# Attention times value by head: two banks of one double, one normalisation, and a new planned order

## The chip, the core and the metric

The kernel runs on one core of a Trainium2 chip. TensorE (PE) multiplies matrices into PSUM, VectorE (DVE) and ScalarE (ACT) work elementwise and can read PSUM, GpSimd (POOL) works on SBUF, and SyncE (SP) issues most DMAs. Each engine runs its own list of instructions in order and waits on semaphores for the others. The metric is the device time of one execution, in microseconds; the median of three runs of the kernel before is 265.42.

## The reference

Two layers, one behind the other. The first is attention with a block mask: 4 batches, 8 heads, 768 positions, head size 64. The mask keeps blocks of 32 x 32: neighbours, the first and last block row and column, and three drawn blocks for each block row. The second is x @ w_in, then h * sigmoid(beta * h), then @ w_out, on 3072 tokens.

```python
scores = scale * np.matmul(q, k.transpose(0, 1, 3, 2))
scores = np.where(mask, scores, -1000000000.0)
scores = scores - np.max(scores, axis=-1, keepdims=True)
attn = np.exp(scores)
attn = attn / (np.sum(attn, axis=-1, keepdims=True) + 1e-09)
out = np.matmul(attn, v)
...
h = x @ w_in
g = h * (1.0 / (1.0 + np.exp(-beta * h)))
return (g @ w_out).astype(np.float32)
```

## The kernel before

**Units.** Heads are taken in pairs, 16 pairs in all (x), four for each batch. The queries of a batch are cut into a tile of 256 and one of 512 (n), so there are 32 units of one pair and one tile. A unit has score steps ("sc", line 602): each fills one *double* of PSUM, a tile "sc" of two banks with 512 columns each, one bank for each head. Head 0 stands in rows 0 to 63 of kX and qX and head 1 in rows 64 to 127, so a score product uses 64 of PE's rows, and those of the two heads stand in the list one behind the other. ACT takes the exponential of a whole double into "et" ("ex", line 621), and DVE multiplies it by the mask ("mk", line 626). The first four units (N_PEMASK) have the mask added on PE instead, by products of shut_qk and onehot. There are four doubles, eight banks.

**Attention times value (add_tail, line 653).** For each 128 queries and each head, six products of 128 rows and 65 columns (64 of v and a column of twos that yields the sums) add up in one bank ("mm" is a single bank, half of a double). Two groups of 128 queries times two heads share a bank. So a unit of 256 queries has one such step "av" of 24 products, and one of 512 has two ("half"). DVE then takes the reciprocal of the four sums ("rc", line 679) and multiplies ("nm", line 682) into xst. From there xst is transposed into x, in the first eight units and the last pair by PE, otherwise by a transposing DMA of SP.

**The second layer (add_moe, line 741).** Groups of 256 or 512 tokens: "hp" is x @ w_in (four products of 512 or 256 columns), "th" a tanh on ACT, "gm" the gate on DVE. Five of the groups are done with fewer products through sums and differences of halves ("sg", "pr", add_mixed, line 824), the first one and the last differently sized.

**Loads.** k, q and v come by SP's DMAs into st, are cast to half precision by DVE or POOL (add_cast, line 523), and k and q are then transposed: by PE for the first four pairs, by a DMA of SP (line 544) for the other twelve.

**Order.** The order of all this is written out. STEPS (line 43) lists node numbers in the order of emission, each with its engine letter and the slots of the buffers that it takes. in_steps (line 163) reads it. A token such as 1x192V2 puts one zero matmul of 192 columns into bank 2; besides these, four stand in emit_first (line 390). A token such as 176P5:171 puts two steps together (in_halves, line 317): each is done as products of 64 rows, the first node with rows 0 to 63 and the second with rows 64 to 127 in turn; at the later token of the pair the row halves change over. Between the two an empty instruction of POOL is told to wait for the last product of each half, and the second run waits for it. Where a POOL cast is emitted, it is told to wait for the DVE instruction emitted last before it (line 1021).

**Banks.** Tile dependencies are kept for each double; class Banks (line 204) takes away those between different banks of a double.

Of the kernel before, what the change touches and what calls it, by code (L numbers as in the profile page):

```python
# [10 lines left out]
FP32 = mybir.dt.float32  # L11
# [12 lines left out]
class Node:  # L24


    def __init__(self, kind, eng, dur, lat, emit, deps=(), take=(), use=(), moved=0,
# [11 lines left out]
        self.first, self.mark = False, None  # L39
# [4 lines left out]
0D 1V2 1x192V2 1P4 30S3 34S5 16S6 12S1 13G0 17G4 38S 44S0 31D3 39G 32P7 35D5 1x192V2 36P0 24S 20S 48S6  # L44
3A 1x192V2 8P6 33D2 6P1 7D 25G 21G 1V2 18P3 14P7 15D0 37A 2A 9A 19A 2x192V6 89P2 90Ab 1x256V1 40P0
1x256V1 78P1 79A4 41D 1x256V1 91P3 93P0 4P4 22P2 26P3 94Ad 45G3 49G6 46P5 27D 5D 82P0 2V3
1x128V3 50P4 23A 92A5 80P1 58S3 54S7 28S5 72G 29G3 42S4 64S1 73G 74G 47D1 51D 83A7 81Aa 1x448V0
100P3 101A3 102P2 103A6 104P0 105A0 52S8 53G1 59D0 68S3 55D3 75G 76G 77G 56P3 57D3 60P2 61D 84P6
115P1 116A9 113P2 111P0 65D0 66P7 43D0 85D3 95P3 112A4 62S6 86D0 67D 87P2 88D2 191P0 194P3 114A7
192Ae 96De 97D0 188P2 69D5 106P3 70P0 71D 63G2 10P1 98P2 11D 99D 107D0 108D4 195A1 193D 196D  # L50
185P3 189A3 186A6 211P0 1V2 1x256V2 182P2 1x320V3 117P2 118D3 119D0 2V3 1x448V3 109P2 197P3
120P3 212Aa 214P0 183A4 208P2 190D 110D 121D 131P3 198A0 122P6 137P7 209Ac 217P2 187D 199D 184D
200P2 123A1 132A3 124D1 143P6 133D 210D 215A9 138A2 201D2 202D4 128P1 140P3 125P0 218A2 134P4
146P2 203P5 129A1 216D 139D 213D 130D 126A3 127D 144A4 145D 135A6 147A0 141A5 220P3 221A0 238G4
234G6 235S 223P0 136D 155P4 156A3 204D8 205D 142D 158P5 159A6 224A6 164P7 206P3 161P6 162A2 148D
219D 149P2 157D 160D 222D 150A3 245P0 246A5 152P4 167P5 168A1 165A0 153A4 225D 163D 226P6 251P0
252A8 207D2 151D 248P1 249Ae 169D 229P5 227Da 166D 228D1 285P3 154D 257P0 170P4 258A1 253D 230De
231D 247D 250D 176P5:171 288P1 260P0 259D 286A2 287D 365D 366D 361D 236D0 239S 242G5 171P 254P3
172P:177 289A4 279P1 261Ad 294P0 177P 178P:173 243S 237S0 271S2 255Ab 256D 291P3 295Ac 262D
282P0 173P 280A9 296D 290D 240D5 281D 241S 179P 292A0 293D 263P7 283A7 266P3 272G2 232P1 284D  # L60
297P2 300P0 180A0 174A1 233A 402P2 367D 264Da 362D 265D3 244G1 267Dh 268D 269P1 298D1 299D0
301Dc 302D 405P3 270D 303P0 304D 403Aa 363D 364D 404D 411P1 408P2 406A6 274S4 277S6 305S5 273S3
308S8 311S7 275D4 276S 427S2 313P1 409A7 410D 412A8 413D 314A3 315D1 306G3 322P6 319P7 323A0
324D 407D 278G3 312G2 309G0 428G4 417P2 414P1 418A9 415Ae 416D 320A5 321D 331P0 316P1 317A3
332A1 318D 333D 328P4 329A0 330D 334P5 335A4 336D 325P3 326A2 435P3 436A0 438P0 337P2 340P4 419D
420P5 439Ab 444P3 441P0 338A6 327D 369D0 437D 341A3 346P3 339D 421D8 349P2 422D0 352P5 445Ac
442A2 447P0 450P3 342D 343P4 350A6 446D 347A2 443D 351D 423P2 348D 440D 355P3 448A4 449D 424Dd
425D 451A3 452D 353A3 354D 430S4 433S0 307S2 310S 181S 175S 466P3 460P0 358P2 344A4 434G0 431G3
345D 453P5 456P4 356A1 461Ad 463P0 357D 359A5 454Dh 360D 475P1 467Aa 469P3 457D3 455D1 464A3
375P5 472P0 376P 470A8 476A9 429S1 432S 485P3 491P1 372D 373D 468D 462D 458D 471D 378P4 379P  # L70
473A1 488P0 492Ac 497P1 486Ab 465D 474D 477D 481P7 478P6 489A7 494P0 498A6 500P1 495Ad 501A9
368D 377D0 380D 482D1 370D 487D 386P 597P0 598Ae 387P:383 479D2 480D3 493D 483D 499D 496D 502D
591P3 594P1 383P 604P0 617S1 620S6 426S1 459S 592A2 595Aa 607P3 608A8 605A0 384P 385A 618D1 490D
506P3 503P2 625P3 621D5 371D 623S4 638S5 388A1 626A9 610P0 611Ad 641S0 639G2 374D 504D9 505D1
389P 390P 628P3 629A3 507Dg 508D 631P1 632A5 652P0 653A1 381D 382D 593D 392P 393P 596D 599D 627D
612D 600P6 646P0 644S7 619S0 659S3 484S 642G0 394D 633D 601D7 602D4 606D 647Aa 509S 513P74:510
649P1 650A4 510P 511A4 622S 667P0 662S1 665S2 680S5 640S2 683S6 686S8 668A2 670P1 516P6 609D
660D6 391D 395P 671A6 630D 648D 669D 517A3 663G4 512D0 518D 528P0 522P1 525P2 519P3 529A1 530D
514A5 515D 643S 523A6 524D 526A1 520A0 672D 527D 673P3 688P0 674Ae 396P 531P4 397A 689Ab 661S3
664S 398S 681G1 682S1 521D 634P3 635D5 654D 636D1 532A3 690D 533D 691P3 694P0 692Ac 695A5 613P2  # L80
614Db 684D0 651D 615D2 675D 537P3 538A3 701P3 704P2 702A8 645G1 703D 705A7 534P1 549P0 550A4
543P6 546P5 540P7 539D 535A6 552P2 706D 624G3 666G2 551D 544A5 547A2 541A3 553A1 536D 545D 555P3
542D 685S 603S0 616S 399S 401S 714P3 707P0 548D 655P4 556A5 708Ad 676P5 715A1 720P0 696D 554D
557D 717P1 677Dc 558D0 561D 678D2 564P6 565P 656Db 657D4 808P2 718A6 811P1 721A3 814P0 567P7
809A2 693D 697P5 568P 812A0 815Aa 566A0 817P1 687D0 560D 563D 562D 698De 699D0 823P2 820P0 818A9
559D 709D 572P 569D 710P3 575P 824A5 821Ac 833P0 858S4 861S6 658S 679S 722D 716D 711Dc 712D3
836P2 839P1 834Ad 576P 719D 571D 723P1 573P 810D 400S 577D1 724Dc 864S8 637S 725D1 840A7 837Ae
845P2 848P0 849A1 842P1 570D 581P 582P 574D 578P 846A3 579P 866P2 713S 891S5 813D 825D 841D 822D
892D2 869P0 843A4 872P1 867Ab 847D 583D 726S 700S 730P7 727P5 873A8 733P3 819D 816D 844D 826P2
829P4 731A1 728A5 870A6 580D 584P 850D 874D 729D1 894S0 895G5 859G0 732D 734A3 585P 827D7 828D3  # L90
735D 830Df 831D 860S2 838D 835D 586D 590S 589S 878P0 875P1 739P4 736P7 879A5 881P0 876Aa 880D
877D 862G3 863S 897S4 899P1 924S6 587S 927S7 893S3 588S 740A2 745P6 737A6 882A9 741D 748P4 746A4
900A0 749A3 751P0 752A1 738D 851P1 747D 871D 905P3 760P32:742 906Ac 750D 852Dc 902P2 742P 911P3
903A2 753D 883D 853D2 761A2 743A4 908P2 854P1 909A4 762D 868D 855D5 744D 856D 907D 910D 772P0
773A0 912Ad 766P3 763P5 757P2 764A1 769P6 754P7 865G3 913D 928G4 925G3 765D 914P2 774D 1013P0
832S1 857S 896S 926S0 930S1 929S 1038S2 767A3 768D 758A4 759D 884P3 887P2 770A6 755A5 915A7
1014A1 1028P2 1029Aa 771D 756D 1019P3 885D6 886D0 1016P0 781P3 904D 888Db 889D 784P2 1020Ab
1022P3 1017A5 785P:782 1025P2 1058P0 782P 1023A9 1026A6 1049P3 775D0 901D 778D 1015D 780D 916D
917P4 920P5 783A0 776D 1027D 779D 789P 786D 918D0 919D2 921D4 922D 1050Ae 1059A4 1021D 1030D
1060D 1051D 1046P3 1047A3 792P:790 1052P2 1053Ac 890S 1041S6 1071P0 1061P3 790P 1055P2 793P  # L100
1062A2 777D 1018D 1044S8 923S 932P7 947P6 1072A0 1056A7 1074P0 962P4 933A1 948A2 1075Ad 788D
1024D 1042D2 934D0 1057D 1073D 1048D 1034P7 1031P1 938P5 963A4 949D 950P6 944P0 1032D9 931G0
794D1 1033D2 964D 935P4 787D 798P 799P 953P1 951A5 952D 939A0 940D 1054D 1035D3 936A2 945A5 937D
1036D 946D 1076D 791A 800D 804S 959P4 941P6 954A6 1039G4 1045G1 898D2 955D 1040S1 1043S 805S
956P2 795P 960A4 961D 942A1 957A6 1083P2 943D 1077P3 1080P0 796P 1084Aa 1078A6 958D 971P4 968P2
1081Ab 969A0 1063D 980D0 970D 1082D 797D 977P1 974P6 1064P5 972A1 965P2 801P 975A0 976D 978A5
# [40 lines left out]
HOP = 60.0  # L147
# [911 lines left out]
```

## Time and profile before

| | |
|---|---|
| runs, us | 265.65, 265.42, 264.58 (median 265.42) |
| profiled execution, span | 265.9 us |
| ACT, exponentials | 144, 139.7 us busy |
| DVE, masks | 132, 83.0 us busy |
| PE, x @ w_in of 512 columns | 304 of 128 rows, 70.4 us busy |
| PE, attention times value | 1152, 42.6 us busy |
| DMA, mean | 138 GB/s |

How to read the rows: a group's row has the engine, the operation, what it writes and reads, the shapes, the count, busy time and the mean length of one in ns, and after the bar the idle time of the engine before them with what ended it. For PE the shape begins with rows * columns of the array that are used. A row of the timeline has its start and its length in us; consecutive equal instructions are merged. Matmuls overlap, so the length of one (269 ns, say) is longer than the distance from one to the next. PEld is the loading of weights. A row of the table by stretch has the stretch, its length, the busy time of PE, PEld, DVE, ACT and POOL, the granted clock, the DMA share and GB/s. In the chain, "PE sc L198" is PE's matmuls (line 198 is a recording helper), and the number behind the start is how long the chain ran there.

### The profile page before, as it was taken

To read this page: it belongs to the slowest core of one execution; us is meant where nothing else is said; L and a number is where in the kernel's file an instruction comes from. 1 tells how busy PE (TensorE), PEld (TensorE's weight loads), DVE (VectorE), ACT (ScalarE), POOL (GpSimd) and SP (SyncE) were. 2 spreads that over 40 slices of the span, in tenths; PEclk is the share of its full clock that TensorE was granted. 3 is DMA by queue.
4 is the path that set the end of the run, shared out by engine and by line. 5 is a ranking of instruction groups with operands and counts; after the bars stand their busy time and mean duration, and the time that the engine had idled before them with its cause. 6 is when DMAs were issued, how large, how long until landed. Compare 5 with 4: busy or idle time off the path is not lost.

```text
span 265.9 us, 7061 instructions
## 1 busy us (share of the span) xinstructions
PE 257.2 (97%) x2899; PEld 168.6 (63%) x2899; DVE 227.7 (86%) x477; ACT 211.2 (79%) x284; POOL 35.6 (13%) x56
## 2 busy tenths in 40 slices
PE   8999999999998999799999999999999999999995
PEld 3575674644455875546776446766567886568884
DVE  4277999999998899599999889999879789778872
ACT  5699999889997989798976999994868876674331
POOL 4482000116020111140002103001200000000000
PEclk9999999999999999999999999999999999999999
DMA  6899994699739579625441597910504103110042
GB/s 186 285 248 232 200 215 161 138 284 258 150 59 271 138 182 271 158 67 184 127 99 55 138 257 179 237 25 0 129 11 121 22 2 120 31 42 0 5 156 79
DMA packets 50131, 36.70 MB, mean 138 GB/s; under 512 B 29732, under 2 KB 46644, under 8 KB 50100
## 3 DMA queue, kind: packets, MB, share of 16 engines
q1 hardware_dynamic: 46368, 32.06, 46.2%
q0 software_dynamic: 3664, 4.19, 9.3%
q8 instruction: 22, 0.36, 0.6%
q14 instruction: 9, 0.07, 0.1%
q10 hardware_dynamic: 68, 0.01, 0.0%
HBM read 27.27 MB, written 6.29 MB: 126 GB/s over the span
## 4 chain that ended last, share of the span: by engine, by line
PE 72%; DVE 9%; DMA 6%; ACT 5%; issue 4%; SPq 1%; POOL 1%; DVEq 0%; ACTq 0%; POOLq 0%
PE sc L198 72%; DMA qX<-s 4%; DVE et L198 4%; ACT et L198 3%; DMA st<-in_v_dram 2%; ACT t_sb L198 1%; DVE w_mix L198 1%; DVE xst L198 1%; DVE s L198 1%; SPq L504 1%; DVE g L198 1%; SPq L544 0%; DVE qX L198 0%; POOL va L198 0%; POOL s L198 0%
## 5 line engine op out<-in xcount | busy, mean ns | idle before, releaser
L198 ACT ACTIVATE et<-sc 128x1024 f16<-128x1024 f32 x144 | 139.7, 1039 | 16.6 <-PE sc L198 14.6
L198 PE MATMUL sc<-x,w_in_sb 128*128 128x512 f16 (+2 forms) x464 | 90.7, 350 | 0.2 <-DVE g L198 0.2
L198 DVE TENSOR_TENSOR et<-et,mask 128x960 f16<-128x960 f16 x132 | 83.0, 663 | 0.6 <-ACT et L198 0.6
L198 ACT ACTIVATE t_sb<-sc,beta_c_sb 128x512 f16<-128x512 f32 (+1 forms) x112 | 65.3, 640 | 22.6 <-PE sc L198 18.0
L198 DVE SCALAR_TENSOR_TENSOR g<-t_sb,sc 128x512 f16<-128x512 f16 (+1 forms) x112 | 63.8, 603 | 9.5 <-ACT t_sb L198 9.1
L198 PEld LDWEIGHTS <-w_in_sb 128*128 128x128 f16 (+1 forms) x464 | 41.7, 97 | 38.3 <-issue 5.8
L198 PEld LDWEIGHTS <-g 128*128 128x128 f16 (+1 forms) x552 | 47.9, 98 | 19.0 <-issue 8.0
L198 PE MATMUL sc<-w_out_sb,g 128*128 128x256 f16 (+3 forms) x432 | 51.8, 286 | 0.0
L198 PE MATMUL sc<-qX,kX 64*128 64x256 f16 (+1 forms) x384 | 47.8, 329 | 3.5 <-DMA qX<-s 3.1
L198 PEld LDWEIGHTS <-et 128*128 128x128 f16 x1152 | 40.4, 97 | 6.7 <-issue 2.5
L198 PE MATMUL sc<-va,et 128*128 128x65 f16 x1152 | 42.6, 193 | 0.0
L198 PEld LDWEIGHTS <-kX 64*128 64x128 f16 x384 | 17.2, 95 | 19.6 <-issue 13.7
L198 POOL CAST s<-st 128x768 f16<-128x768 f32 (+2 forms) x22 | 17.0, 784 | 82.0 <-DVE g L198 49.1
L198 PEld LDWEIGHTS <-s 128*128 128x128 f16 (+1 forms) x264 | 20.4, 98 | 5.8 <-issue 1.9
L198 PE MATMUL sc<-w_mix,s 128*128 128x256 f16 (+1 forms) x216 | 23.8, 272 | 0.1
L198 DVE TENSOR_TENSOR xst<-sc,recip 128x256 f16<-128x256 f32 x48 | 19.9, 420 | 1.0
L198 POOL CAST va<-st 128x768 f16<-128x768 f32 x13 | 11.5, 893 | 50.6 <-DVE recip L198 18.7
L198 DVE TENSOR_TENSOR osb<-osb,sc 128x512 f32<-128x512 f32 (+2 forms) x19 | 11.7, 616 | 4.8 <-PE sc L198 3.6
L198 ACT COPY osb<-sc 128x512 f32<-128x512 f32 (+3 forms) x17 | 8.8, 535 | 7.6 <-PE sc L198 6.5
L198 DVE RECIPROCAL recip<-sc 128x4 f32<-128x4 f32 x48 | 8.2, 174 | 5.5 <-PE sc L198 5.3
L198 PE MATMUL sc<-w_mix,g 128*128 128x256 f16 (+2 forms) x96 | 10.9, 264 | 0.0
L198 PE MATMUL sc<-g 128*128 128x512 f16 (+5 forms) x24 | 8.2, 426 | 1.3 <-DVE mask_blk L379 1.2
(59 smaller groups left out, 97.6 us busy)
## 6 DMA issues: line engine op xcount, KB each, us to landing
st<-in_v_dram SPq DMA_DIRECT2D x16, 384.0 KB, 5.5
out_dram<-osb SPq DMA_DIRECT2D x23, 256.0 KB, 2.3
st<-in_k_dram SPq DMA_DIRECT2D x14, 384.0 KB, 4.2
st<-in_q_dram SPq DMA_DIRECT2D x14, 384.0 KB, 5.0
w_out_sb<-in_moe_w_out_dram POOLq DMA_DIRECT2D x2, 1024.0 KB, 20.5
w_in_sb<-in_moe_w_in_dram POOLq DMA_DIRECT2D x2, 512.0 KB, 7.7
w_in_sb<-in_moe_w_in_dram POOLq DMA_DIRECT2D x1, 1024.0 KB, 13.2
st<-in_k_dram SPq DMA_DIRECT2D x4, 128.0 KB, 3.0
```

The source lines that it names most:

```text
L198: r = f(*a, **kw)
L504: nc.sync.dma_start(out=at(st)[:, :, lo * D:hi * D], in_=rows[:, :, lo * D:hi * D])
```

## The change

Attention times value is now one step for each head, written into that head's bank of a double; both heads' results are normalised by one reciprocal and one product for the whole unit. The recip buffer grows to hold four groups. A unit of 512 queries has two steps of 24 products, one of 256 has two of 12. A step can be crossed in halves of 64 rows with another, as steps of the second layer could before. STEPS is new throughout: 1316 nodes against 1332, no zero-matmul tokens, and 19 pairs of crossed steps against 9. Four of these are the two heads of one unit (units 2, 11, 18 and 25).

```diff
-        self.first, self.mark = False, None
+        self.first, self.half, self.fresh = False, None, False
...
 STEPS = """
-0D 1V2 1x192V2 1P4 30S3 34S5 16S6 12S1 13G0 17G4 38S 44S0 31D3 39G 32P7 35D5 1x192V2 36P0 24S 20S 48S6
...
-1326A 1331S
+34S8 30S0 16S2 12S7 38S 35G6 0D 20S 36P3 44S4 1P6 54S3 17G1 31D4 32P2 2A 24S 18P7 33D0 37A 3A 48S8
...
+1309P 1307D 1311P6 1313S 1310A 1312D 1315S
 """
...
-def banks_of(b):
-
-    return (2 * b.slot, 2 * b.slot + 1) if b.pool == "sc" else (b.slot,)
+def banks_of(b, n):
+
+    if b.pool != "sc":
+        return (b.slot,)
+    return (2 * b.slot, 2 * b.slot + 1) if n.half is None else (2 * b.slot + n.half,)
...
-        "recip": many(persist, "recip", [P, 2, 2, 1], FP32),
+        "recip": many(persist, "recip", [P, 2, 4, 1], FP32),
...
-            Tap.into = node.bank
+            Tap.into = node
...
-        xs = Buf("xst")
-        last = None
-        for half in range(nq // 2):
-            ab, rb = Buf("mm"), Buf("recip")
-
-            def av_ap(ab=ab):
-                return at(ab)[:, 0:4 * (D + 1)].rearrange("p (i h d) -> p i h d", i=2, h=2)
-
-            def av(half=half, av_ap=av_ap):
-                a = av_ap()
-                for i in range(2):
-                    qc = half * 2 + i
-                    for hh in range(2):
-                        for kc in range(NC):
-                            at0 = (kc % kn) * n + (qc % CG) * (n // CG) + qc // CG * P
-                            pe.matmul(
-                                a[:, i, hh, :],
-                                lhsT=at(ets[kc // kn])[:, hh, at0:at0 + P],
-                                rhs=at(va)[:, hh, kc, 0:D + 1],
-                                start=(kc == 0), stop=(kc == NC - 1))
...
+        xs, ab, rb = Buf("xst"), Buf("sc"), Buf("recip")
+        wide = nq * (D + 1)
+
+        def av_of(hh):
+            return at(ab)[:, hh, 0:wide].rearrange("p (i d) -> p i d", d=D + 1)
+
+        def av_ap():
+            return at(ab)[:, :, 0:wide].rearrange("p h (i d) -> p h i d", d=D + 1)
+
+        heads = []
+        for hh in range(2):
+            def terms(hh=hh):
+                for qc in range(nq):
+                    for kc in range(NC):
+                        at0 = (kc % kn) * n + (qc % CG) * (n // CG) + qc // CG * P
+                        yield (av_of(hh)[:, qc],
+                               lambda r, kc=kc, at0=at0: at(ets[kc // kn])[r, hh, at0:at0 + P],
+                               lambda r, kc=kc: at(va)[r, hh, kc, 0:D + 1],
+                               qc == 0 and kc == 0, D + 1)
+
+            def av(terms=terms):
+                whole = slice(0, P)
+                for i, (o, l, w, start, _) in enumerate(terms()):
+                    pe.matmul(o, lhsT=l(whole), rhs=w(whole), start=start,
+                              stop=i % NC == NC - 1, skip_group_check=True)
+            a = add("av", "PE", 32 * nq * NC, 180, av,
+                    deps=masked + [cv] + [(h, -180 - HOP) for h in heads],
+                    take=[] if heads else [ab], use=ets + [va] + ([ab] if heads else []))
+            a.terms, a.bank, a.half, a.fresh = terms, ab, hh, True
+            heads.append(a)
+
+        def rc(eng):
+            dve.reciprocal(out=at(rb)[:, :, 0:nq], in_=av_ap()[:, :, :, D:D + 1])
+
+        def nm(eng):
+            dve.tensor_tensor(
+                out=at(xs)[:, 0:nq].rearrange("p c h d -> p h c d"), in0=av_ap()[:, :, :, 0:D],
+                in1=at(rb)[:, :, 0:nq].to_broadcast([P, 2, nq, D]), op=ALU.mult)
+        r = add("norm", "DVE", 85 + 2 * nq, 80, rc, deps=heads, take=[rb], use=[ab])
+        last = add("norm", "DVE", 65 + 133 * nq, 80, nm, deps=[r], take=[xs], use=[ab, rb])
...
-                    banks.access([x[0] for x in log if x[1] is m.bank], "PE",
-                                 banks_of(m.bank), m.bank in n.take, m)
+                    banks.access([x[0] for x in log if x[1] is m], "PE",
+                                 banks_of(m.bank, m), n.first and (m.fresh or m.bank in n.take), m)
```

More of the change, by code (lines that the diff above doesn't have):

```diff
@@ L47 @@
[L47 to L58, printed above, removed]
@@ new lines @@
+116P0 53G0 105A6 118P3 43G1 117Ab 77G 119A8 63G3 5D 9D 84P1 85P 114P2 86D0 87D3 66P0 88P1 67D
+115A9 89D0 195P1 198P0 70P6 71D 196Ae 96P2 97P 199Aa 192P1 98Dd 108P3:109 99D4 197D 189P2 193Ad
+109P 186P0 110D1 190Ac 111D0 120P1 112P6 121P 113D 187A0 213P2 122D9 123D2 100P6 10P7 101D 214A2
+124P2 11D 125D 201P3 191D 216P1 202A7 126P4 194D 210P0 215D 127A0 132P6 211A4 128D0 129P7 200D
+150P5 133A0 212D 141P1 217A9 135P4 134D 188D 138P0 130A1 144P3 142A0 131D 136A4 143D 219P3 151A6
+153P2 137D 220A3 152D 147P1 203D 222P2 145A5 221D 234G5 204P3 223A1 218D 238G7 235S 205P 139A4
@@ new lines @@
+424S2 427S1 413P1 279D 263P2 414Aa 264P 178A1 399A1 295P1 265Dh 266D3 296P 184A0 400D 410P0 297D3
+404P3 273G5 411Ae 267P4 276G0 274S 405A9 302G1 298D2 268D 299P5 401P1 300D 407P0 360D 309P4 402A4
+362D 408A2 403D 363D 312P5 315P6 310A3 318P2 422G3 316A0 327P3 244G2 406D 423S2 319A4 425G6 321P0
+328A2 303S1 428G3 311D1 317D 320D 409D 313A0 330P4 329D 322A6 324P1 331A4 323D 435P1 325A5 305G4
+429P3 333P0 430A5 308G1 332D 314D 306S 326D 438P2 436A6 432P3 431D 336P1 426S 415D 433A8 342P2
+437D 337A4 185S 412D 348P3 334A1 338D 343A5 335D 441P3 345P1 349A3 434D 439A7 350D 351P0 344D
@@ new lines @@
+442Ab 339P3 440D 352A5 443D 444P2 416P3 417P 346A0 353D 445A3 347D 340A2 452P0 418D4 419D1 354P2
+453Ac 446D 455P2 355A6 341D 458P3 447P0 459A0 365D0 448P 356D 368D 456Ad 464P1 461P3 465A4 374P4
+457D 454D 462A7 467P1 460D 371P5:375 468A1 449D0 450D3 487P3 366D 488A2 481P0 484P1 375P 469D
+482A9 466D 475P3 463D 372P 476Aa 369D 478P0 485A6 477D 470P3 364D 479Ae 471P 378D 373A0 490P1
+472Dd 367D 585P0 491A3 379P 473D0 376D 586A0 593P3 582P1 607S8 610S5 613S6 179S 480D 382P 583A5
+483D 486D 618P0 594A8 380P:383 619A7 579P1 621P3 608G0 492D 489D 383P 622Ab 377D 494P0:493 384D1
@@ new lines @@
+580A4 615P3 629S2 632S7 370D 493P 616A1 637P1 420S2 474S 635S1 651S4 654S0 451S 609S0 655G2 611D4
+495De 496D2 388P 381A 657S3 638Ac 652D5 497S 385P:389 581D 587D 643P1 653S1 640P3 644Ad 596P0 584D
+633D0 389P 641A2 630G3 612S 599P1 390D 386P 597A3 631S2 645D 588P3 589P 600A6 498P0 590D5 620D
+591D1 394S 623D 516P1 499A2 504P4 500D0 517A1 518D 659P3 673S8 634S 505A0 662P1 513P0 395S 663A9
+676S2 674G4 598D 387D 501P1 656S 660Aa 642D 665P1 514A2 506D 675S3 507P6 502A5 639D 519P4 595D
+508A4 503D 666Ae 510P7 677G0 515D 391P 509D 511A3 678S 520A6 636G2 681P0 687P1 512D 617D 688A0
@@ new lines @@
+672S 850S6 650S 628S 396S 397S 704P 680G3 548D 563P:561 828A6 706Da 707D3 714D 816P2 864P0 817A0
+810P3 561P 558D 717D 811A4 858P2 853S2 856S5 881S3 884S7 694S 887S0 854G3 564P 708S 562A 851G1
+559D 821D 809D 865A8 718P3 719P 565A1 720D7 721D1 859A5 818D 566P 567P:569 722S 806D 861P0 812D
+862A7 852S0 842P3 839P2 569P 843A2 570P 840A1 815D 723P1 571D 568D 836P3 841D 724A2 576S 833P2
+726P3 829D 837A9 844D 747P0 834Ab 838D 572P 748A0 835D 727A3 822P3 725D1 728D 823P 749D 870P2
+756P3:573 824D8 871A0 825D0 882G0 867P0 889P3 912S8 915S4 575S 868A3 732P45:729 832D 883S2 863D
@@ new lines @@
+796D 968D0 1042A4 798P 801S 1068Ad 944P1 799D 802S 1183P1 1069D 945A5 1058P2 959P6 1184A3 919G3
+800S 1030S6 965P7 960A2 1023S1 1059A8 953P0 966A6 1031G2 946D 1043D 1037D 961D 956P1 969D 954A1
+967D 962P2 957A2 955D 1061P2 963A3 958D 1051P3:1050 1062A9 964D 1081P0 1050P 971D 1082Aa 1070P1
+1052Dd 974P45:977 1053D2 1071Ab 1084P0 1093P3 1085A6 977P 970D 1083D 1186P1 1094A4 1197P0 972D
+975P 1066D 1198A5 978P 1080D 1063D 976A0 1072D 1087P3 1090P0 1199D 1088A1 982P 1060D 1091A7 983P
+979D 973D 1187Ac 1073P3 1074P 984A 1054S 803S 1189P0 1225P1 1075D2 1076D4 1190A2 985P:988 981D
@@ new lines @@
+1077S 1211P3 1226A8 1214P0 988P 1089D 1215A9 1200P1 1092D 980D 989P:986 1201Ab 1216D 1217P0 1086D
+986P 1212Ad 1095D 1203P1 987D1 1096P3 1204Ae 990D 1097P 991P 1098D2 1218A1 1099D1 1228P1 1202D
+1231P3 1229A0 992P 1188D 1219D 1232A4 1100P0 994P 1101D 1213D 1102P2 993D 1191D 1220P3 1103A5
+1221P 1108P3 1120P1 1230D 1185D 1233D 1222Dg 1223D3 1105P5 1121A3 1104D1 1122D 1192P3 1193P 1135P0
+1106A3 1136A4 1227D 1147P1 1132P2 1194Dg 1195D0 1205D 1137D 995P 1196S0 1206P3 996D 1109A1 999S
+1224S 1207P 1123P0 1107D 1208D1 1110D 1114P4 1124A5 1000S 1125D 1209D0 998S 1148A0 1126P5 997S
@@ new lines @@
+1133A4 1149D 1210S 1117P3 1127A3 1115A2 1234P3 1235P 1118A0 1144P1 1236D0 1116D 1129P0 1237D4
+1119D 1138P4 1134D 1130A1 1145A5 1111P6 1139A2 1128D 1238P5 1141P7 1239A 1146D 1131D 1112A6 1240P5
+1113D 1150D0 1243P0 1241A0 1249P1 1142A4 1270P6 1242D0 1276P2 1143D 1279P3 1261P5 1140D 1255P7
+1271A4 1267P4 1262A5 1272D 1250A2 1268A0 1156P6 1269D 1151D 1157P 1251D 1153D 1258P4 1158A1 1159P1
+1263D 1280A1 1277A4 1154D 1256A3 1160P 1244A6 1155D 1259A2 1164P 1165P 1260D 1162D 1282P4 1161D
+1152D 1246P5 1166D 1167P 1283A0 1168P 1170P 1163D 1169D0 1245D 1171P 1278D 1285P0 1281D 1173P
@@ L657, in add_tail @@
         nq = n // P
-        xs = Buf("xst")
-        last = None
-        for half in range(nq // 2):
-            ab, rb = Buf("mm"), Buf("recip")
-            def av_ap(ab=ab):
-                return at(ab)[:, 0:4 * (D + 1)].rearrange("p (i h d) -> p i h d", i=2, h=2)
-            def av(half=half, av_ap=av_ap):
-                a = av_ap()
-                for i in range(2):
-                    qc = half * 2 + i
-                    for hh in range(2):
-                        for kc in range(NC):
-                            at0 = (kc % kn) * n + (qc % CG) * (n // CG) + qc // CG * P
-                            pe.matmul(
-                                a[:, i, hh, :],
-                                lhsT=at(ets[kc // kn])[:, hh, at0:at0 + P],
-                                rhs=at(va)[:, hh, kc, 0:D + 1],
-                                start=(kc == 0), stop=(kc == NC - 1))
-            def rc(eng, rb=rb, av_ap=av_ap):
-                dve.reciprocal(out=at(rb), in_=av_ap()[:, :, :, D:D + 1])
-            def nm(eng, half=half, rb=rb, av_ap=av_ap):
-                dve.tensor_tensor(
-                    out=at(xs)[:, half * 2:half * 2 + 2], in0=av_ap()[:, :, :, 0:D],
-                    in1=at(rb).to_broadcast([P, 2, 2, D]), op=ALU.mult)
-            a = add("av", "PE", 790, 180, av, deps=masked + [cv], take=[ab], use=ets + [va])
-            r = add("norm", "DVE", 100, 80, rc, deps=[a], take=[rb], use=[ab])
-            last = add("norm", "DVE", 345, 80, nm, deps=[r, last], take=[xs] if half == 0 else [],
-                       use=[ab, rb] + ([xs] if half else []))
@@ L1023 @@
                 if b.pool in BANKS:
-                    banks.access([x[0] for x in log], n.on, banks_of(b), b in n.take, n)
+                    banks.access([x[0] for x in log], n.on, banks_of(b, n),
+                                 n.fresh or b in n.take, n)
 def n_default(f):
```

100 lines of the change are left out of this document (30 added, 70 removed).

## The prediction

> **What bounds the kernel now.** I read the page's shares first, then busy time by stretch, then the chain that ended last, then the waits.
>
> ```profile
> span 265.9 us, 7061 instructions
> PE 257.2 (97%) x2899; PEld 168.6 (63%) x2899; DVE 227.7 (86%) x477; ACT 211.2 (79%) x284; POOL 35.6 (13%) x56
> ...
> 30.00:60.00 30.00, 29.86 (x376) 18.69 (x375) 29.26 (x68) 27.79 (x42) 2.96 (x6) 1.00 0.90 200
> 60.00:108.00 48.00, 45.31 (x516) 27.93 (x514) 45.87 (x89) 44.88 (x57) 8.54 (x10) 1.00 0.81 188
> ...
> 155.00:253.00 98.00, 97.97 (x1090) 67.97 (x1086) 85.60 (x169) 72.09 (x101) 5.21 (x6) 1.00 0.31 79
> ```
> ```profile
> 80.90 19.01 PE sc L198 x284
> ...
> 108.60 46.68 PE sc L198 x524
> ...
> 155.30 98.33 PE sc L198 x1090
> ```
> ```profile
> PE sc L198 <- DMA qX<-s: 3.1, 2, 1.6
> ...
> PEld L198 <- POOLq L332: 1.0, 5, 0.3
> ```
>
> PE sets the end. From 155 to 253 us it is busy 97.97 of 98, and the chain runs through it unbroken from 155.30. DVE is nearly as full only up to about 108 us, and even there PE idles little: 0.14 us from 30 to 60, 2.69 from 60 to 108. What DVE or ACT saves therefore shortens nothing by itself; what counts is PE's own work, its few waits, and the start. The one large wait is for two transposing DMAs, 3.1 us. Both look alike:
>
> ```profile
> 74.53 0.83 POOL L198 CAST va<-st 128x768 f16<-128x768 f32 x1 [9.39 <-DVE g L198]
> ...
> 75.29 0.83 POOL L198 CAST s<-st 128x768 f16<-128x768 f32 x1
> ...
> 76.15 1.21 SPq L544 DMA_TRANSPOSE qX<-s  x1
> ...
> 80.90 0.61 PE L198 MATMUL sc<-qX,kX 64*128 64x512 f16 x4 [1.62 <-DMA qX<-s]
> ```
> ```profile
> 104.04 0.83 POOL L198 CAST s<-st 128x768 f16<-128x768 f32 x1 [5.09 <-DVE et L198]
> ...
> 106.21 1.56 SPq L544 DMA_TRANSPOSE qX<-s  x1
> ...
> 108.60 0.40 PE L198 MATMUL sc<-qX,kX 64*128 64x256 f16 x4 [1.52 <-DMA qX<-s]
> ```
>
> A cast of q on POOL waits for a DVE instruction that stands before it in the program, the transpose is issued behind it, and 5.6 us after the cast's start (4.6 in the second case) the scores can run. PE, in order, has nothing else.
>
> **The change part by part.** I counted both programs' instruction lists, which the planned order fixes.
>
> *PE's arithmetic.* Columns are the same. The prices:
>
> ```profile
> 74.55 1.69 PE L198 MATMUL sc<-va,et 128*128 128x65 f16 x48
> ...
> 76.17 0.82 PE L198 MATMUL sc<-qX,kX 64*128 64x512 f16 x6
> ...
> 76.93 1.05 PE L198 MATMUL sc<-w_out_sb,g 128*128 128x256 f16 x8
> ...
> 77.91 0.39 PE L198 MATMUL sc<-qX,kX 64*128 64x512 f16 x2
> ...
> 78.23 1.05 PE L198 MATMUL sc<-w_out_sb,g 128*128 128x256 f16 x8
> ```
>
> A value product takes (1.69 - 0.19)/47 = 32 ns, 0.19 being the row length of one (193 ns, below). A 128-row matmul of 256 columns takes (1.05 - 0.27)/7 = 111 ns; two 64-row ones of 512 run at once in (0.82 - 0.39)/2 = 215 ns. From 77.91 to 78.23 is 0.32 us, 0.10 more than such a pair; 76.93 to 77.91 is 0.98, 0.09 more than eight at 111 ns. So each change between 64-row and 128-row tiles costs about 0.1 us. Without the zero matmuls, which stood in gaps, the list before has 120 such changes and the list after 126: 6 x 0.1 = **+0.6 us**.
>
> *Crossing.* Pairs of steps that run as 64-row halves grow from 9 to 19: four are the two heads of a value product, the rest projections as before. Large ones cost no columns: pairs start together (rows of x2, 0.11 us apart, further down), like one 128-row matmul at 111 ns. For the value products no row exists: 144 matmuls become 288 of 64 rows and 65 columns. At best the two halves overlap wholly (28 ns a pair by columns, 65/256 of 111 ns): -0.5 us. At worst each half takes the 32 ns of a whole: 144 x 32 = +4.6. The nearest row, pairs of 256 columns, overlaps wholly; I take **+0.5**. Each pair also puts an empty instruction into POOL's queue, for which the second half waits. Behind nine of them PE waited 1.0 us; ten more cost 10/9 of that, **+1.1** (0 if all ten hide behind the scores between, +3 at the longest, 0.3 each). No cast stands close before most of these in POOL's list; one behind a cast would wait up to 0.83 us.
>
> [...]
>
> *Normalisation.*
>
> ```profile
> L198 PE MATMUL sc<-va,et 128*128 128x65 f16 x1152 | 42.6, 193 | 0.0
> ...
> L198 DVE TENSOR_TENSOR xst<-sc,recip 128x256 f16<-128x256 f32 x48 | 19.9, 420 | 1.0
> ...
> L198 DVE RECIPROCAL recip<-sc 128x4 f32<-128x4 f32 x48 | 8.2, 174 | 5.5 <-PE sc L198 5.3
> ...
> L198 DVE TENSOR_TENSOR osb<-osb,sc 128x512 f32<-128x512 f32 x15 | 10.2, 682 | 2.7 <-PE sc L198 2.5
> ...
> L198 DVE TENSOR_TENSOR osb<-osb,sc 128x256 f32<-128x256 f32 x3 | 1.3, 419 | 1.4 <-ACT osb L198 1.0 <-PE sc L198 0.4
> ```
>
> 48 reciprocals and 48 products become 32 and 32. A product of 512 should take 420 + (682 - 419) = 683 ns, so each of the 16 large units saves 174 + 840 - 683 = 0.33 us: 5 us at most off DVE. Four casts of 768 and two mask or output copies also leave DVE, mostly for POOL (13% busy). Counted as **0**: DVE ends no large wait of PE; it hides under PE's 97.97 of 98 us. The reverse side: one double stays taken for 683 instead of 420 ns, and small units hold two banks where one did. 16 x 0.26 = +4.2 us if each were exposed.
>
> *Transposes.* By these prices I summed PE's work between the place of each q or k cast in the program and the first score that needs it. Before, the late one at 80.90 has 4.5 us, the one at 108.60 has 8.0, its DMA standing only 0.3 us ahead. After, the smallest is 8.0 for a cast and 4.5 for a DMA, most over 9; DMAs before stand at 0 to 3 us in eight cases. The SP queue has as many entries, 121, reordered with loads earlier. I take both waits as gone, **-3.1**; bounds 0 (they stay) and -3.1.
>
> *Start.*
>
> ```profile
> 4.88 0.82 PE L198 MATMUL sc<-mask_q,onehot 24*128 24x384 f16 x2
> ...
> 5.36 0.74 POOL L198 CAST s<-st 128x256 f16<-128x256 f32 x2 [2.23 <-DMA st<-in_k_dram]
> ...
> 5.63 0.61 PE L198 MATMUL sc<-g 128*128 128x512 f16 x1
> ...
> 7.02 0.39 PE L198 MATMUL sc<-shut_qk,onehot 64*128 64x256 f16 x2
> ...
> 8.10 1.02 ACT L198 ACTIVATE et<-sc 128x1024 f16<-128x1024 f32 x1 [1.14 <-PE sc L198]
> ...
> 10.44 0.42 PE L198 MATMUL sc<-qX,kX 64*128 64x256 f16 x2
> ...
> 10.91 0.27 PE L198 MATMUL sc<-shut_qk,onehot 64*128 64x256 f16 x2
> ...
> 11.02 0.27 PE L198 MATMUL sc<-qX,kX 64*128 64x256 f16 x2
> ```
>
> The two mask products and the zero matmul that stood before the first score are moved back or gone; q's cast then ends last, at 5.36 + 0.74 = 6.10, so with its turn (0.2) the first score can start near 6.3, not 7.02: **-0.7**, as ACT waits for PE then (1.14). Against it stands the clock: a pair takes 0.21 us up to 10.65 and 0.11 afterwards. That is the rival below, bound +3.5.
>
> Sum: +0.6 + 0.5 + 1.1 - 3.1 - 0.7 = -1.6 us on the span of 265.9, so 264.3. The median of the runs, 265.42, lies 0.5 below that span; the forecast for the median is **263.8**.
>
> **The rivals.**
> - *One transpose stays late, or its wait goes elsewhere*: the second stall had a counted lead of 8.0 us as well, and POOL waited 5.09 us for DVE there, which the count does not see. For it: two new leads are no longer than 8.1. Against it: DVE has up to 5 us less. 263.8 + 1.5 = 265.3, no change.
> - *Slower: the clock rises later.* Without the 20 later zero matmuls PE is less full up to 10.65 us. Twelve masked score steps of four pairs and 38 turns, all at the slow clock, need 12 x 0.85 + 38 x 0.107 = 14.3 us, while ACT needs 12 x 0.9 = 10.8: ACT, then everything behind it, falls 3.5 us back, and the 0.7 is lost: 268.0. It decides from the point where the pairs are still at 0.21 us after about 14 us. Against it: a slow PE has no gaps, and would be filled by real work. [...]
> - *Slower: value products in halves or banks.* 4.6 instead of 0.5 gives 267.9; 4.2 us of exposed normalisation 268.0. The point from which it decides: crossed products over 60 ns a pair, or PE waiting for DVE's xst in most units.
> - *The change doesn't bind*: only 4 of 32 units cross heads, so of that alone no more than 4.6 us can show.
>
> **How the numbers follow.** Forecast 0.45, of which 0.08 ends within the bound; late transpose 0.20 (0.13 same, 0.05 slower, 0.02 faster); clock 0.17, and halves or banks 0.13, both slower but for 0.01; a better start than counted 0.05, faster. About 0.5% (264.1 to 266.7) is what a measurement can tell from no change. Together faster 0.44, same 0.22, slower 0.34. The likeliest case's own range is 261.3 to 265.3; with the slower cases, 260.3 to 269.5.
>
> **What would show it.** Right: no wait of PE for qX or kX over 0.5 us, first exponential near 7.4 us, pairs at 0.11 us by 11 us, crossed value products under 40 ns a pair. Wrong: 64-row pairs at 0.42 us long past 11 us; weight loads of et waiting for POOL's queue for more than 2.5 us in sum; PE waiting for xst on DVE; or a new wait for q or k.

## The result, and the profile after

The changed kernel takes 267.49 us (median of 20 runs, 265.29 to 269.54), the kernel before 265.53 us beside it (20 runs, 262.82 to 268.71). The ratio is 1.0077, 95% interval 1.0053 to 1.0100: about 2.0 us slower, where 1.6 us faster was forecast.

The profiled execution of the changed kernel seems to say the opposite. From its page:

```profile
span 263.5 us, 7512 instructions
PE 254.4 (97%) x3131; PEld 167.8 (64%) x3131; DVE 229.0 (87%) x441; ACT 210.6 (80%) x283; POOL 43.8 (17%) x61
```

Its span is 2.4 us shorter than the 265.9 us before. But a run's time is more than its span, by 1.8 us for the changed kernel: this execution is the run of 265.29 us (span 263.5), the fastest of the twenty. For the kernel before it is 1.9 us (264.40 and 262.5 in its second profile, below), so the profile before belongs to a run of about 267.8 us, 2.3 us above that kernel's median. So neither is typical, and they miss in opposite directions.

The stretches of the changed kernel, columns as before:

```profile
30.00:60.00 30.00, 29.08 (x356) 17.44 (x354) 27.49 (x55) 27.57 (x41) 7.04 (x9) 1.00 0.98 237
60.00:108.00 48.00, 47.14 (x602) 28.47 (x601) 46.63 (x81) 45.43 (x58) 8.52 (x10) 1.00 0.76 165
155.00:253.00 98.00, 98.00 (x1176) 69.02 (x1175) 86.75 (x158) 69.75 (x99) 2.78 (x3) 1.00 0.27 59
```

PE still sets the end (98.00 of 98 us at the back), and idles 0.92 us from 30 to 60, where it idled 0.14. What PE waits for (engine, line, releaser: sum, times, longest), in this execution:

```profile
PE sc L196 <- POOL s L196: 1.8, 3, 1.1
...
PE sc L196 <- DVE g L196: 0.8, 2, 0.7
PE sc L196 <- DMA x<-xst: 0.5, 1, 0.5
```

The same for a second profile of the same kernel (span 267.1 us), the first experiment below. Its run of 268.85 us lies 0.9 us above the median of its eight, so its waits are on the long side:

```profile
PE sc L196 <- DMA x<-xst: 3.0, 2, 1.8
...
PE sc L196 <- POOL s L196: 1.0, 3, 0.6
PE sc L196 <- DVE g L196: 1.0, 2, 0.8
PE sc L196 <- DMA w_in_sb<-in_moe_w_in_dram: 0.8, 1, 0.8
```

And for a second profile of the kernel before (run 264.40 us), the last experiment:

```profile
span 262.5 us, 7061 instructions
...
PE sc L198 <- DVE mask_blk L379: 1.2, 1, 1.2
PE sc L198 <- ACT et L198: 0.5, 2, 0.3
PE sc L198 <- DMA qX<-s: 0.4, 1, 0.4
```

Here both large waits for qX are gone without any change, and the span is 3.4 us shorter. They are not part of every execution. The changed kernel has lost them too, but it has a new wait: the second layer stands still for x, 0.5 us in sum in its fastest execution and 3.0 us in the second profile.

### The profile page after: what moved, and what is told of

Same layout as the page of the kernel before. It is cut to its first block, busy times and chain, and to the rows that moved or that the text cites. A ratio compares the mean times of both kernels' runs of the same rounds, so it can differ in the third digit from the quotient of the medians.

```text
span 263.5 us, 7512 instructions
## 1 busy us (share of the span) xinstructions
PE 254.4 (97%) x3131; PEld 167.8 (64%) x3131; DVE 229.0 (87%) x441; ACT 210.6 (80%) x283; POOL 43.8 (17%) x61
## 4 chain that ended last, share of the span: by engine, by line
PE 62%; DMA 17%; DVE 16%; SPq 1%; ACT 1%; issue 1%; POOL 0%; DVEq 0%; POOLq 0%
PE sc L196 62%; DMA w_out_sb<-in_moe_w_out_dram 8%; DVE et L196 6%; DVE g L196 4%; DMA x<-xst 4%; DMA st<-in_v_dram 3%; DMA st<-in_k_dram 2%; DVE xst L196 2%; DVE s L196 2%; SPq L502 1%; DMA kX<-s 1%; ACT et L196 1%; DVE w_mix L196 1%; DVE recip L196 1%; DVE osb L196 0%
## 5 line engine op out<-in xcount | busy, mean ns | idle before, releaser
L196 PE MATMUL sc<-w_out_sb,g 64*128 64x256 f16 (+3 forms) x512 | 56.1, 281 | 0.0
L196 PE MATMUL sc<-qX,kX 64*128 64x256 f16 (+1 forms) x384 | 50.5, 331 | 1.7 <-DVE g L196 0.7
L196 PEld LDWEIGHTS <-et 128*128 128x128 f16 (+1 forms) x1296 | 40.4, 97 | 6.8 <-issue 1.9
L196 PE MATMUL sc<-va,et 128*128 128x65 f16 (+1 forms) x1296 | 42.9, 192 | 0.1
L196 POOL CAST s<-st 128x768 f16<-128x768 f32 (+2 forms) x25 | 23.2, 935 | 73.1 <-PE sc L196 39.8
L196 POOL CAST va<-st 128x768 f16<-128x768 f32 x15 | 13.8, 925 | 61.1 <-PE sc L196 34.0
L196 DVE TENSOR_TENSOR xst<-sc,recip 128x256 f16<-128x256 f32 (+1 forms) x32 | 17.8, 557 | 0.9
L196 PE MATMUL sc<-w_mix,g 128*128 128x256 f16 (+3 forms) x112 | 13.3, 264 | 0.0
L196 DVE CAST s<-st 128x768 f16<-128x768 f32 (+1 forms) x12 | 7.0, 583 | 6.2 <-DMA st<-in_k_dram 3.8
L196 DVE RECIPROCAL recip<-sc 128x4 f32<-128x4 f32 (+1 forms) x32 | 6.1, 192 | 6.0 <-PE sc L196 5.9
```

What stands on the lines that cost most here:

```text
L196: r = f(*a, **kw)
```

## The experiments

Each kernel ran beside the kernel before on the same chip; the medians of the latter were 265.41, 265.27, 265.63 and 265.40 us in the four groups, so ratios are compared where two groups meet.

| kernel | median, us | ratio to before, interval |
|---|---|---|
| the changed kernel again | 267.97 | 1.0089 (1.0050 to 1.0128) |
| with zero products | 267.23 | 1.0051 (1.0018 to 1.0083) |
| before, no zero products | 264.97 | 0.9989 (0.9962 to 1.0016) |
| new order, old value steps | 270.13 | 1.0175 (1.0143 to 1.0207) |
| one entry moved | 267.30 | 1.0080 (1.0046 to 1.0115) |
| five later loads moved | 266.22 | 1.0021 (0.9998 to 1.0044) |
| both (loads first) | 265.10 | 0.9994 (0.9969 to 1.0019) |
| before, with held loads | 270.76 | 1.0224 (1.0176 to 1.0271) |
| whole heads | 267.69 | 1.0100 (1.0059 to 1.0142) |
| loads first, old value steps | 269.82 | 1.0159 (1.0125 to 1.0194) |
| loads first, a cast later | 264.55 | 0.9952 (0.9930 to 0.9974) |
| before again | 265.53 | 1.0010 (0.9971 to 1.0049) |

### Clock, value steps or order

*The changed kernel again*, nothing edited.

> The changed kernel once more, unchanged, for its spread and for a second profile: median 267.5 +- 0.5 us. If its fast execution (265.3 in the first profile) was a lucky start, this profile has a span near 265.7 and differs in the first 30 us; if not, the 2 us lie later, in waits of PE.

It repeats the loss. The span of its profile is 267.1 us, and its waits for x lie near 100 and 141 us, so most of the loss comes later than the first 30 us. It is read further below.

*Zero products put in or taken out.* Edits, in STEPS of the changed kernel and of the one before:

```diff
-... 36P3 ... 32P2 ... 18P7 ... 40P0
+... 1x512V3 36P3 ... 1x192V2 32P2 ... 1x384V7 18P7 ... 3x448V0 40P0
```
```diff
-0D 1V2 1x192V2 1P4 ... 35D5 1x192V2 36P0 ...
+0D 1P4 ... 35D5 36P0 ...
```

> The changed kernel with six zero matmuls back in PE's gaps of the first 8 us. Clock theory (PE is too empty at the start, so the clock rises later): 1 to 2 us faster than the changed kernel, about 266, with a narrower spread. Order theory (the new order loses later, in changes and waits): no difference, 267.5 +- 0.3. Value theory (the two-bank steps cost): no difference either.

> The kernel before without the 20 zero matmuls of its order; the four at the start stay. Clock theory: 2 us slower than before, about 267.5, the pairs of 64 rows at 0.21 us until 12 to 14 us. Order and value theories: as before, 265.5 +- 0.4.

In these profiles PE does speed up earlier with zero products: in the changed kernel the matmuls counted from 10 to 11 us, 12 in each profile, keep PE busy for 0.69 us with them, for the whole microsecond in its two profiles without; in the first of these the pairs of 64 rows and 256 columns reach 0.11 us only at 11.95 us. The granted clock is 1.00 from 0 to 14 us in all of these profiles, with pairs at 0.21 us as with pairs at 0.11, so that it is the clock that rises was the author's reading and is not shown. The time hardly follows. Without zero products the kernel before is not slower, 264.97 us. With them the changed kernel has 267.23 us, whose interval overlaps that of the repeat. So the slow pairs at the start are not what costs the 2 us; a part of up to about 1 us (267.97 against 267.23, and the intervals) can't be excluded.

*The order alone*: the new order, written for the value steps as before.

```diff
-494P0:493 ... 493P ... 495De 496D2
+503P0 ... 506P1 ... 504De 505D2 507De 508D
```

(Unit 11 as an example, in the numbering of before: two steps of one bank, uncrossed, each normalised by itself.)

> The new order with attention times value as it was: two groups of 128 queries and both heads in one bank, one reciprocal and one product for each, no crossing of heads. Value theory: about 265.5, as before. Order theory and clock theory: 267 to 268, as the changed kernel, and DVE 3 to 5 us busier.

At 270.13 us it is slower than the changed kernel, beyond the 267 to 268 expected. So the new value steps are not what made the change slower: within this order they gain. That the order itself loses is not shown by this run alone, as the order was laid out for the new steps; the runs that change only the order, below, show it.

### What the order does to SP's queue

The queue of SP in the second profile of the changed kernel (start, length, operation; SPq is SP's DMA queue), from the timeline:

```profile
74.98 12.90 SPq L718 DMA_TRANSPOSE x<-xst  x2
87.94 0.58 SPq L502 DMA_DIRECT2D st<-in_v_dram  x1
88.56 1.77 SPq L502 DMA_DIRECT2D st<-in_k_dram  x1
90.43 0.41 SPq L502 DMA_DIRECT2D st<-in_q_dram  x1
90.89 1.19 SPq L718 DMA_TRANSPOSE x<-xst  x1
92.19 1.34 SPq L542 DMA_TRANSPOSE kX<-s  x1
93.57 0.58 SPq L502 DMA_DIRECT2D st<-in_v_dram  x1
94.25 1.23 SPq L718 DMA_TRANSPOSE x<-xst  x1
95.62 2.63 SPq L542 DMA_TRANSPOSE kX<-s  x1
```

A transpose issues in 1.2 us (row of 90.89); the first row lasts 12.90 us because the second of its two (node 474, x of unit 10) waits for a normalisation on DVE that ends at about 86.7 us:

```profile
85.98 0.68 DVE L196 TENSOR_TENSOR xst<-sc,recip 128x512 f16<-128x512 f32 x1
```

Every load behind it waits as well: the first of them, of v, is issued at 87.94 us.

By stretch, this profile and, behind it, the second profile of the kernel before:

```profile
75.00:90.00 15.00, 14.72 (x228) 10.59 (x228) 14.93 (x27) 15.00 (x18) 0.22 (x1) 1.00 0.34 65
90.00:108.00 18.00, 16.29 (x251) 10.14 (x248) 15.35 (x27) 14.64 (x19) 2.93 (x4) 1.00 1.07 203
```
```profile
75.00:90.00 15.00, 15.00 (x225) 11.20 (x222) 14.70 (x31) 14.71 (x17) 0.70 (x1) 1.00 0.75 194
90.00:108.00 18.00, 18.00 (x206) 11.94 (x202) 16.55 (x32) 16.81 (x23) 3.72 (x4) 1.00 0.87 225
```

The DMA engines move 65 GB/s where they moved 194, then their busy share is 1.07, where it was 0.87. The transposing DMA of x for unit 11, issued at 94.25 us into that crowd, releases PE only at 100.79, 6.5 us later. From PE's timeline of the second profile:

```profile
98.75 0.81 PE L196 MATMUL sc<-x,w_in_sb 128*128 128x512 f16 x3
100.79 2.10 PE L196 MATMUL sc<-x,w_in_sb 128*128 128x512 f16 x9 [1.23 <-DMA x<-xst]
...
139.26 0.59 PE L196 MATMUL sc<-x,w_in_sb 128*128 128x512 f16 x2
141.63 0.61 PE L196 MATMUL sc<-x,w_in_sb 128*128 128x512 f16 x2 [1.78 <-DMA x<-xst]
```

(The expectations call these two waits 1.4 and 1.9 us; by the rows they are 1.23 and 1.78.) The wait at 141 us repeats the pattern: node 672 (x of unit 16) holds SP until 123 us, six loads follow it from 124 to 133 us, and x of unit 19, issued at 136.8 us, releases PE only 4.8 us later.

The held queue is in the fastest execution too, the first profile of the changed kernel, but there it costs little (SP, then PE):

```profile
74.39 12.91 SPq L718 DMA_TRANSPOSE x<-xst  x2
```
```profile
98.84 2.10 PE L196 MATMUL sc<-x,w_in_sb 128*128 128x512 f16 x9 [0.47 <-DMA x<-xst]
```

Near 141 us that execution has no wait for x. So a held queue doesn't cost the same each time: x of unit 11, issued at 93.28 us here, releases PE after 5.6 us instead of 6.5.

*One entry moved.*

```diff
-420S2 474S 635S1 651S4 654S0 451S 609S0
+420S2 635S1 651S4 654S0 451S 474S 609S0
```

> The changed kernel with one entry of SP's queue moved: the transposing DMA of x for unit 10 (node 474) stands behind the loads of k of units 14 and 15 instead of ahead of them. Queue theory (this entry waits for a normalisation that ends at 86.7 us, and everything behind it in SP's queue, four loads of 384 KB among it, is held from 75 to 86.7 us; bunched afterwards, the loads and the transposes slow one another, so that x for unit 11 takes 6.5 us to land and PE waits 1.4 us for it near 100 us, and 0.7 us for a crossing that stands behind a cast near 97): both waits go, 1.4 + 0.7 = 2.1 us less at most, median 265.9 to 266.8, the DMA share from 75 to 90 us rises from 0.34 to above 0.6. Rival (the second layer simply stands too close behind the normalisation in the new order, whatever the loads do): the wait near 100 us stays, 267.6 +- 0.5.

The wait near 100 us is gone and the DMA share from 75 to 90 us is 0.60, as the queue theory says; the time is not what it says, 267.30 us. In the profiled execution (268.5 us, 1.2 above the median) what was won is given back 40 us later (timeline, then stretches):

```profile
137.04 0.59 PE L194 MATMUL sc<-x,w_in_sb 128*128 128x512 f16 x2
139.58 0.67 PE L194 MATMUL sc<-x,w_in_sb 128*128 128x512 f16 x2 [1.95 <-DMA x<-xst]
```
```profile
138.00:140.00 2.00, 0.42 (x2) 0.11 (x2) 2.00 (x4) 0.00 (x0) 0.00 (x0) 1.00 0.67 128
140.00:144.00 4.00, 4.00 (x13) 1.25 (x13) 2.12 (x4) 2.52 (x3) 0.00 (x0) 0.57 0.89 316
```

PE waits 1.95 us for x of unit 19, as it did before the edit (1.78), and then runs at half the clock for some 3.4 us (0.50 from 141 to 143 us, a mean of 0.57 over 4 us). Only three of the twelve runs have a mean clock under 0.995; the median of the other nine is 266.6 us. So the lost clock explains this execution and at most a part of the median; why the rest of the gain is missing stays open.

*Both, and the later loads alone.* To the edit above, or without it:

```diff
-679S7 521D 592S0 ... 672S 850S6 650S ... 858P2 853S2 856S5 881S3 884S7 694S 887S0
+679S7 521D 853S2 856S5 887S0 592S0 ... 850S6 881S3 672S 650S ... 858P2 884S7 694S
```

> As the kernel with one entry moved, and also the five loads of units 21 and 22 that stood behind the transposing DMA of x for unit 16 (node 672, waiting until 123 us) moved ahead of it or of that for unit 12. Queue theory: besides the waits near 97 and 100 us the one near 141 us (1.9 us for x of unit 19) shrinks below 0.5 us: 3.5 us less than the changed kernel at most, median 264.0 to 265.5, at or below the kernel before. Rival (distance between normalisation and second layer): the wait near 141 us stays, 267.5 +- 0.7.

> The changed kernel with only the five loads of units 21 and 22 moved ahead, node 474 left where it is. If the two stretches of held loads cost independently: the wait near 141 us (1.9 us in the repeat of the changed kernel) goes, that near 100 us (1.4 us) stays: 265.8 +- 0.5. If the second alone decides (what is won near 100 us is lost again at 141 us, as the kernel with one entry moved suggests, 267.3): 265.1, as with both.

With both, the second layer no longer waits for x (timeline of that kernel):

```profile
98.52 2.75 PE L194 MATMUL sc<-x,w_in_sb 128*128 128x512 f16 x12
...
137.52 1.03 PE L194 MATMUL sc<-x,w_in_sb 128*128 128x512 f16 x4
```

Six entries of one queue moved, nothing computed otherwise, and the loss is gone: from 1.0077 and 1.0089 to 0.9994, some 2.3 us. The later loads alone bring most of it, 1.0021; what the first entry adds to them (0.0027) is within the overlap of the two intervals, and alone it brings nothing that can be measured. The 266.22 us of the later loads alone lie in the range given for two independent costs, but the first entry alone doesn't fit it. The runs are also closer together, 264.37 to 266.33 us.

*The fault put into the kernel before.* Its transposing DMA of x for unit 10 (node 484), and with it the one of x that stood ahead of it (node 426), are put ahead of loads:

```diff
-617S1 620S6 426S1 459S ... 659S3 484S ... 509S
+426S1 484S 617S1 620S6 459S ... 659S3 ... 509S
```

> The kernel before with the same fault put in: the transposing DMA of x for unit 10 (node 484, whose normalisation ends at about 86 us) stands ahead of the loads of unit 13 instead of behind those of unit 14, so that SP's queue is held from about 76 to 86 us. Queue theory: PE waits for x or for qX between 90 and 110 us, 1 to 3 us longer than the kernel before: 266.5 to 268.5. Rival (loads have enough slack, the loss of the changed kernel is elsewhere): 265.4 +- 0.5.

5.5 us slower by the medians, more than expected. SP, DVE and PE of that kernel, then its clock:

```profile
76.35 10.53 SPq L708 DMA_TRANSPOSE x<-xst  x2
...
91.33 0.56 DVE L194 CAST s<-st 128x768 f16<-128x768 f32 x1 [3.97 <-DMA st<-in_k_dram]
91.80 0.65 DVE L194 TENSOR_TENSOR et<-et,mask 128x960 f16<-128x960 f16 x1
...
92.51 2.77 PE L194 MATMUL sc<-va,et 128*128 128x65 f16 x47 [3.87 <-DVE et L194]
```
```profile
90.00:92.00 2.00, 0.00 (x0) 0.00 (x0) 0.68 (x2) 0.90 (x2) 0.00 (x0) 0.75 1.03 324
92.00:98.00 6.00, 5.49 (x65) 4.37 (x66) 4.76 (x11) 1.94 (x2) 0.83 (x1) 0.52 1.12 326
98.00:100.00 2.00, 2.00 (x25) 1.44 (x23) 2.00 (x5) 0.75 (x1) 0.00 (x0) 1.00 1.16 310
```

Here it isn't x that is late but a load: its cast stands on DVE ahead of a mask, the mask waits with it 3.97 us, and the value products behind the mask 3.87 us. From 90 to 98 us the clock is at half for 6.8 us in sum (0.75 over 2 us, 0.52 over 6), most of it after PE had started again. Held loads reach PE along more than one way. The expectation had the direction, but neither the way nor the size.

### Halves, normalisation, and a better version

*Whole heads*: the four crossed value steps uncrossed.

```diff
-108P3:109 ... 494P0:493 ... 493P ... 705P0:704 ... 704P ... 1051P3:1050 ... 1050P
+108P3 ... 493P0 ... 494P ... 704P0 ... 705P ... 1050P3 ... 1051P
```

> The changed kernel with the four crossed pairs of value products uncrossed: each head as 24 (or 12) products of 128 rows, the same order else. If the halves ran at 28 ns a pair, as the trace of the changed kernel has it, uncrossing brings back 32 ns for each of 144 products, +0.6 us, and takes away four empty instructions of POOL, each at most 0.3 us: 267.0 to 268.3, no difference that can be measured. If the halves were what made the change slower (32 ns each half), -4 us: 263.5.

267.69 us, no difference. Crossed and whole value products side by side, from the timelines of the changed kernel's first and second profile:

```profile
196.15 0.92 PE L196 MATMUL sc<-va,et 64*128 64x65 f16 x48
196.91 0.38 PE L196 MATMUL sc<-qX,kX 64*128 64x512 f16 x2
```
```profile
97.99 0.92 PE L196 MATMUL sc<-va,et 128*128 128x65 f16 x24
```

48 halves take as long as 24 wholes, and in both the next work starts 0.76 us after the first: 32 ns a pair, not the 28 of the expectation.

*Loads first, old value steps.* The order of the kernel with six entries moved, with the value steps as before:

```diff
-494P0:493 ... 493P ... 474S 609S0 ... 495De 496D2
+503P0 ... 506P1 ... 484S 619S0 ... 504De 505D2 507De 508D
```

> The order with the six moved entries, with attention times value and its normalisation as before (one bank for each two groups of 128 queries, 48 reciprocals and 48 products, nothing of it crossed). The same exchange in the order without the moves made it 2.2 to 2.6 us slower. If that is the price of the old value steps in this order (DVE's longer normalisation exposed): 267.0 to 268.0. If it was an accident of the held loads (the old value steps met x transposes at other moments): 265.1 +- 0.6.

By the ratios (1.0159 and 0.9994) 4.4 us slower than with the new ones, more than expected. Its first wait, and the same releaser in the kernel with the new steps:

```profile
PE sc L181 <- DVE xst L181: 3.7, 9, 0.7
```
```profile
PE sc L194 <- DVE xst L194: 0.4, 2, 0.3
```

By these two profiles 3.3 us of the 4.4 are PE waiting for the longer normalisation; the rest was not taken apart. It is an upper bound on the worth of the new steps, as this order was laid out around them.

The same pair of runs limits what was said of the queue. With the old value steps, the six moved entries change the ratio only from 1.0175 to 1.0159, within the intervals. In the kernel with the old steps and the loads still held (the order alone, above) SP's queue stands as long, and from 75 to 90 us the DMA engines move 76 GB/s, yet PE never waits for x in its profile:

```profile
75.75 13.73 SPq L695 DMA_TRANSPOSE x<-xst  x2
```

So the 2.3 us of the six entries hold for the new value steps in this order; they are no fixed price of a held queue. The new steps in the order of before were not tried: that order has single banks free where they need a double.

*A cast later.* With loads first, PE's largest wait in the profile, beside one of 1.2 us in the first 2 us, is one of 1.2 us at 42 us: DVE's cast of k of unit 5 finds DVE idle for 1.81 us before it, two gates stand behind the cast, PE behind them.

```diff
-251P3 236D1 166A0 ... 170D 237S0 229P 252Ab 167D 173D 283P1
+251P3 166A0 ... 170D 229P 252Ab 167D 173D 236D1 237S0 283P1
```

> As the kernel with the six entries of SP's queue moved, and also the cast of k of unit 5 on DVE (node 236), with its transposing DMA (node 237), moved behind the next two gates and a mask step (nodes 167, 170 and 173). In the trace of that kernel this cast waits 1.8 us for a load (38.9 to 40.7 us), the gates wait behind it in DVE's queue, and PE waits 1.2 us for them at 42 us. If that wait is on the path that sets the end: 0.5 to 1.2 us less, 264.0 to 264.7, below the kernel before. Rival (PE's wait moves on to the next thing, the scores of unit 8 that need this transposed k): no change, 265.1 +- 0.4.

264.55 us, 0.5% under the kernel before, the fastest of these kernels, as the first expectation says; the interval still touches that of the kernel without this move (0.9974 and 0.9969). PE's scores at that place start at 41.03 us with no wait in this profile.

*The kernel before again*, nothing edited:

> The kernel before once more, for a second profile of it. If its two waits for transposed q (1.6 us at 80.9 us and 1.5 us at 108.6 us in the first profile, whose span of 265.9 us stands for a run of about 267.7 us) belong to every execution, both are there again, 3.1 us in sum. If the first of them is an accident of slow executions, as the same order without zero matmuls suggests (one wait, 1.3 us), only the second is there, with a span near 263.5 us.

Neither outcome: both waits are gone, with a span of 262.5 us. Its lines stand in the section on the result; the 0.4 us for qX that is left lies at 53.8 us.

## Why the prediction was wrong

*The step that failed* is "Transposes", in two ways. "I take both waits as gone, -3.1" took two waits of one execution, 2.4 us above the median of 265.42, for the kernel's own. The second profile has neither, and its run is 1.0 us under the median of 265.4; by this one run, an estimate of what they cost on average is about 1 us. And "The SP queue has as many entries, 121, reordered with loads earlier" read the queue by its list. Loads do stand earlier, but behind a transpose that cannot go yet. Leads were counted for q and k only; those of x, which the new order issues into the crowd, were left out, so the sum has no term for them. In this kernel it is +2.3 us, by the six moved entries.

*The base.* "The median of the runs, 265.42, lies 0.5 below that span": a run of this kernel is 1.9 us above its span, so the profiled execution was 2.4 us above the median. The two waits (3.1 us) are most of the 3.4 us between its span and that of the second profile. Half a microsecond was passed on where nearly the whole excess belonged to the waits that the next step took away.

*Start*: the first exponential starts at 6.38 us (forecast 7.4, before 8.10). But the pairs reach 0.11 us only at 11.95 us, not by 11 as the sign of being right had it. Not in the sum was DVE's cast in front of the gates: moving it lowered the ratio by 0.0042, 1.1 us.

*Crossing*: +0.5 for the halves was nothing that can be measured, 32 ns a pair. For the empty instructions of POOL, +1.1 was counted for ten more; weight loads wait 1.1 us for POOL's queue in six cases in the first profile now and 1.8 us in seven in the second, where they waited 1.0 in five before. So 0.1 to 0.8 us came of it.

*Normalisation*: DVE's work for it fell from 28.1 to 23.9 us, 4.2 of the 5 us given as the most:

```profile
L196 DVE TENSOR_TENSOR xst<-sc,recip 128x256 f16<-128x256 f32 (+1 forms) x32 | 17.8, 557 | 0.9
L196 DVE RECIPROCAL recip<-sc 128x4 f32<-128x4 f32 (+1 forms) x32 | 6.1, 192 | 6.0 <-PE sc L196 5.9
```

DVE in sum is no lighter for it: 229.0 us against 227.7; the masks alone take 2.0 us more (85.0 against 83.0). So the "up to 5 us less" that the prediction set against a late transpose did not come about. Counting the normalisation as 0 fits the order before, whose second profile names no wait of PE for xst. In the new order with loads first, the new value steps are worth 4.4 us; the order depends on them, and the sum has no term for that.

*The rivals.* Clock at the start: not the 2 us, by the zero products. Halves: no, by the whole heads. Banks: no, as PE waits 0.4 us for xst in both profiles. "One transpose stays late, or its wait goes elsewhere" had the right mechanism, with 1.5 us as its price; the wait went to x, not q, and cost more. Slower was given 0.34, and 267.5 lies inside the range of 260.3 to 269.5, for reasons that the range was not built on: that it does is luck.

Put together anew from the median of 265.5: about -1.0 (qX), +2.3 (x behind held loads), +1.1 (cast before gates) gives 267.9, against 267.5 and 268.0 measured. This is no independent test: the last two terms were measured on the changed kernel itself, and the first is an estimate from one run. The tile changes (+0.6) and the start (-0.7) would cancel and were not measured alone.

## What to carry to other kernels

An entry's place in a queue tells when it may go, not when it goes (SP stood 12.90 us at two transposes, where one issues in 1.2 us): ask of every entry what it waits for, and what stands behind it. A transposing DMA whose input is late belongs behind loads that could go now, and a cast of a load behind elementwise work that PE needs; how much that is worth has to be measured in the kernel at hand, as the first was worth 2.3 us with one form of the value steps and next to nothing with the other, and the second 1.1 us. And take two profiles before counting a wait as the kernel's own: compare the span (plus what lies around it) with the median first.

## What was not expected of the hardware

Two of the waits of PE cost twice. Just after an idle stretch of 1.95 us (one entry moved) and within one of 3.87 us (held loads in the kernel before) the granted clock fell to 0.50, for about 3.4 and 6.8 us; after 1.78 us in the second profile of the changed kernel it stayed at 1.00. Of the 64 runs of the five kernels with the new order's later loads held, 8 have a mean granted clock under 0.9965, and six of these took 268.5 us or more; of the 42 of the four kernels with these loads moved, none has. But the kernel before, whose loads are not held, has 6 such runs of 88, so that held loads cause it is suggested, not shown. The spread of the changed kernel, 265.29 to 269.54 us, shrinks to 263.77 to 265.13 in the best version.
